# Attention, soft MoE and SoLU on one core: second weights of four late experts summed in one PSUM tile per column block

## The chip, the cores and the metric

The kernel runs on one NeuronCore of one Trainium2 chip. The metric is the device time of one execution in microseconds (us). Five engines work side by side, each through its own list of instructions in order: TensorE (PE in the profile, with its weight loads apart as PEld), VectorE (DVE), ScalarE (ACT), GpSimd (POOL) and SyncE (SP), which issues nearly all the DMAs. They wait for each other through semaphores.

## The reference

Three stages on 8 x 576 = 4608 tokens of width 512 (8 heads of 64).

```python
def sm_attn(qq, kk, vv):                       # softmax attention
    ...
p_packed = sm_attn(p, k, v)                    # 32 packed rows per head
out = sm_attn(q, p_packed, p_packed)           # x: 4608 x 512

logits = x @ phi                               # 4608 x 32, 8 experts x 4 slots
d = softmax(logits, axis=0)                    # dispatch, over the tokens
slot_input = d.T @ x                           # 32 x 512
for e in range(8):
    h = np.maximum(slot_input[e] @ w1[e], 0.0) # 4 x 1024
    slot_out[e] = h @ w2[e]                    # 4 x 512
x = softmax(logits, axis=1) @ slot_out         # 4608 x 512

h = x @ w_in                                   # 4608 x 1024
solu = h * softmax(h)
out = (layer_norm(solu) * g_ln) @ w_out        # 4608 x 512
```

w1 and w2 are 8 x 512 x 1024 and 8 x 1024 x 512 in fp32, 33.5 MB together. w_in and w_out come in 64-bit numbers and are unpacked on the chip.

## The kernel before

It has three stages. In the first, the two attentions run batch by batch while k, v, q and the first weights stream in; it ends with `SIT`, the dispatched slot inputs (line 923), which needs the maximum and the sum over all tokens and so the last batch. The second stage computes the experts. In the third, 36 tiles of 128 tokens go through w_in, the SoLU, the layer norm and w_out.

**Loads.** All bulk loads go through SP's one queue in a fixed order: k, v, q and w_in by batch, then expert weights with w_out among them. Expert weights come as 29 tiles of 128 x 2304 fp32 (1152 KB), each of nine "granules" of 128 x 256 (128 KB); 256 granules hold w1 and w2 of the eight experts. Tile 27 is loaded in three pieces (`CUTS`, line 222) and the last, tile 28, has four granules. Tiles sit in a ring of 14 buffers and a second ring of 3. A load is issued when PE has read the tile that was in its buffer. The order of the granules is set in `_layout` (lines 1649 to 1654): w1 of expert 0, then w1 of e+1 and w2 of e for e = 0 to 4, w1 of 6 and 7, and last w2 of experts 5, 6 and 7 in another arrangement: four column blocks k of 128 columns, in each block the four granules of each of the three experts.

**Experts.** `mk_w1` (line 1000) multiplies `SIT` by the 16 granules of w1 of an expert (L1008), ACT applies the relu (L1019, `hs`), PE transposes it (L1024) and ACT copies it out (L1028, `hT`, 128 x 2 x 4 x 32: all 32 slots are carried through each expert, and only the expert's own four are used in the end). `mk_w2` (line 1044) does the second product for experts 0 to 4 (L1055), copies the PSUM tile to `so` (L1066), transposes it (L1070) and copies the four slot columns into `SO` (L1039). The last NL = 3 experts go through `mk_block` (line 1084) for each block k and expert e: eight matmuls into a PSUM tile of its own (L1097), a copy to `so` on ACT (L1108), a small matmul that transposes, sums four partition groups and picks the expert's four slots (L1114, 128 x 4 columns), and after the third expert a copy of the 12 columns into `SO` (L1039). An fp32 matmul of the program shows as two instructions in the trace.

**SO times w_in.** `sw = SO @ w_in` is summed over four 128-row chunks c into two PSUM tiles n (L1317); chunk c waits for block k = c of the late experts. Then ACT and DVE write `swr` (L1325, L1329), and stage three begins with L1381. In stage three a tile costs PE 16 matmuls on L1520 and 8 on L1526.

**What sets the order.** The instructions of stages one and two are put in order by `Plan`, a list scheduler: every step has an estimated length, dependencies and buffers that it takes and gives back (`caps`, line 256: `w` are four PSUM banks, `h` the `hT` buffers). It tries 250 random variations of the priorities and keeps the best by a weighted sum of three planned times (lines 1342 to 1344). Any change of a step or a latency so gives another order in the whole of stages one and two. Matmuls of zeros (L374) fill PE where the plan sees it idle before `sw` begins.

Of the kernel before, what the change touches and what calls it, by code (L numbers as in the profile page):

```python
# [9 lines left out]
FP32 = mybir.dt.float32  # L10
# [11 lines left out]
class Plan:  # L22
# [10 lines left out]
        "PE": {"PE": 30, "DVE": 200, "ACT": 200},  # L33
# [146 lines left out]
def pack_attention__soft_moe__solu_kernel(  # L180
# [39 lines left out]
    NL = 3  # L220
# [20 lines left out]
    with ExitStack() as p12, tc.manual_schedule():  # L241
# [15 lines left out]
                     "h": 4, "u": 2, "x": 3, "c3": 1}, LOOK1, CALM1, REST1)  # L257
# [691 lines left out]
        def phase2():  # L949
# [6 lines left out]
            W["sw"] = [wp.tile([96, 512], FP32R, name=f"swr{n}") for n in range(2)]  # L956
# [3 lines left out]
            W["SO"] = wp.tile([128, 4, 3, 32], FP32, name="SO")  # L960

        def phase3():
# [3 lines left out]
            W["lo"] = wp.tile([128, 8, 512], FP16, name="wlo")  # L966

# [9 lines left out]
        def first(e):  # L977
            return max(0, 32 * e - 16) if e < NE - 1 else LATE - 16
# [7 lines left out]
        def stream(g0, g1, pe, ns, deps, acq, rel):  # L986
# [11 lines left out]
            return deps[0]  # L998

        def mk_w1(e):  # L1000
# [25 lines left out]
            def act2():  # L1026
                hT = hT_t[e] = W["k"].tile([128, 2, 4, 32], FP32, tag="hT", name="hT", bufs=4)
                nc.scalar.copy(  # L1028
                    hT, ps_t.pop(("ht", e))[:, 0:256].rearrange("p (j g s) -> p j g s", j=2, g=4)
                )  # L1030

            x = stream(first(e), first(e) + 16, pe, NS1, [o_2, o_w1.get(e - 1)], ["w", "h"], [])
            o_w1[e] = x
            x = op("ACT", 264, act, [x], rel=["w"])
            x = op("PE", 214, tr, [x], acq=["w"])
            o_hT[e] = op("ACT", 330, act2, [x], rel=["w"], urgent=10 ** 5)
# [7 lines left out]
        def mk_w2(e):  # L1044
# [19 lines left out]
            def act():  # L1064
                so_t[e] = W["k"].tile([128, 128], FP32, tag="so", name="so", bufs=3)
                nc.scalar.copy(so_t[e], ps_t["s", e][:, 0:128])  # L1066
# [11 lines left out]
            x = op("ACT", 200, act, [x], rel=["w"])  # L1078
            x = op("PE", 107, tr, [x], acq=["w"])
# [4 lines left out]
        def mk_block(k, e, dep):  # L1084
            s0 = LATE + 4 * (NL * k + e - NE + NL)

            def pe(g0, g1):
                def go():
                    if g0 == s0:
                        ps_t["b", k, e] = bank()  # L1090
                    for i in range(g0, g1):
                        for c in range(2):
# [5 lines left out]
                                out=ps_t["b", k, e][32 * a:32 * a + 32, 0:128],  # L1098
                                lhsT=hT_t[e][:, j, g, :],
                                rhs=gran(i)[:, 128 * c:128 * c + 128],  # L1100
                                start=(q == 0),
                                stop=(q == 1),
# [3 lines left out]
            def act():  # L1106
                so_t["b", k, e] = W["k"].tile([128, 128], FP32, tag="so", name="so", bufs=3)
                nc.scalar.copy(so_t["b", k, e], ps_t.pop(("b", k, e))[:, 0:128])  # L1108

            def tr():  # L1110
                if e == NE - NL:
# [575 lines left out]
```

## Time and profile before

| | us |
|---|---|
| time, median of 3 runs | 403.19 (402.27 to 403.28) |
| span of the profiled execution | 400.4 |
| PE busy in it | 379.8 (95%) |
| DVE, ACT, POOL busy | 272.8, 234.5, 209.5 |

The profile shows one more execution, of which only the span is given, from its first to its last instruction; the median of the runs is 2.8 us longer. Times in the trace count from the span's start. By them stage two begins at about 128 us and stage three at about 185 us. The DMA engines are busy throughout until about 175 us of the span, at about 410 GB/s.

### The profile page before, as it was taken

Reading aid. Unit: us, or ns where it says so; the run is one execution under the profiler, and the core shown is the slowest. Engines: PE = TensorE matmul, PEld = TensorE weight load, DVE = VectorE, ACT = ScalarE, POOL = GpSimd, SP = SyncE. Lnnn points to the kernel's source line nnn. Section 1 sums busy time; section 2 is a strip of 40 time slices with the busy share of each in tenths; the row PEclk is TensorE's granted clock in tenths of the full one; section 3 lists DMA queues with packets and bytes.
Section 4 is the critical chain, followed back from the end, with each engine's and each line's share of the span. In section 5 each row is a group of like instructions: output and inputs, shape, how many; then the busy total and the mean of one; then the engine's idle time right before and its main releaser. Section 6 shows DMA issues by size and latency. Waiting matters only on the chain.

```text
span 400.4 us, 9700 instructions
## 1 busy us (share of the span) xinstructions
PE 379.8 (95%) x3788; PEld 200.1 (50%) x3788; DVE 272.8 (68%) x562; ACT 234.5 (59%) x444; POOL 209.5 (52%) x310
## 2 busy tenths in 40 slices
PE   8889899989989999799999999999999999999996
PEld 3456455565545675453444444444444444444445
DVE  1267889689976826945987766767767676676631
ACT  1457777868645743324986656665566566655620
POOL 1024536055331583693778665566665765667540
DMA  8999999999999999950167855776556665767572
GB/s 300 410 419 406 418 410 415 411 418 414 407 419 410 407 420 419 418 199 1 33 145 160 164 133 129 140 152 153 133 118 150 138 139 121 156 148 127 121 157 80
DMA packets 91438, 99.28 MB, mean 248 GB/s; under 512 B 76160, under 2 KB 76800, under 8 KB 85888
## 3 DMA queue, kind: packets, MB, share of 16 engines
q1 hardware_dynamic: 91104, 98.58, 75.8%
q8 instruction: 30, 0.49, 0.5%
q14 instruction: 16, 0.13, 0.1%
q10 hardware_dynamic: 288, 0.07, 0.1%
HBM read 70.85 MB, written 9.44 MB: 201 GB/s over the span
## 4 chain that ended last, share of the span: by engine, by line
PE 71%; DMA 12%; DVE 10%; ACT 3%; issue 2%; SPq 1%; POOL 1%; DVEq 0%; ACTq 0%; POOLq 0%
PE o L1520 29%; PE o L1526 14%; DMA r<-w 5%; PE h L1381 4%; DMA r<-kT 3%; DMA r<-qT 3%; PE sc L390 3%; PE w L1008 3%; PE sw L1317 2%; PE w L374 2%; PE w L473 2%; PE w L1097 2%; DVE bsum L582 2%; DVE bmx L562 2%; PE w L1055 1%
## 5 line engine op out<-in xcount | busy, mean ns | idle before, releaser
L1520 PE MATMUL o<-whi,th 128*128 128x512 f16 x280 | 106.1, 379 | 0.4 <-DMA th<-hi 0.3
L1520 PE MATMUL o<-wlo,th 128*128 128x512 f16 x280 | 106.1, 379 | 0.0
L1490 POOL TENSOR_TENSOR lo<-x,hi 128x1024 f16<-128x1024 f32 (+1 forms) x37 | 77.3, 2092 | 29.8 <-ACT hi L1468 28.1
L1520 PEld LDWEIGHTS <-th 128*128 128x128 f16 x560 | 54.6, 98 | 66.4 <-DMA th<-hi 0.8
L1526 PE MATMUL o<-whi,tl 128*128 128x512 f16 x280 | 66.5, 380 | 0.0
L1430 ACT ACTIVATE e<-s3t,nv 128x1024 f32<-128x1024 f32 x36 | 41.3, 1148 | 40.1 <-DVE nmean L1424 40.0
L1468 ACT ACTIVATE hi<-s3t,nr,rs 128x1024 f16<-128x1024 f32 x35 | 43.4, 1240 | 24.2 <-POOL nr L1451 24.0
L1411 DVE SCALAR_TENSOR_TENSOR s3t<-h,e 128x1024 f32<-128x1024 f32 (+1 forms) x37 | 43.9, 1190 | 17.4 <-ACT e L1402 17.3
L1389 DVE TENSOR_REDUCE nm<-h 128x1 f32<-128x1024 f32 (+1 forms) x37 | 43.9, 1190 | 11.5 <-PE h L1381 11.4
L1460 DVE TENSOR_SCALAR x<-s3t,nmean,rs 128x1024 f32<-128x1024 f32 x35 | 28.8, 824 | 25.4 <-POOL rs L1447 25.3
L1402 ACT ACTIVATE e<-h,nm 128x1024 f32<-128x1024 f32 (+1 forms) x37 | 39.9, 1079 | 5.7 <-DVE nm L1389 3.3
L1526 PEld LDWEIGHTS <-tl 128*128 128x128 f16 x280 | 24.9, 98 | 34.3 <-issue 8.3
L1381 PE MATMUL h<-swr,cT 96*128 96x512 f32 x72 | 28.9, 483 | 1.2 <-DVE swr L1329 0.9
L374 PE MATMUL w<-wz 128*128 128x512 f16 x91 | 26.3, 379 | 3.9 <-ACT A2T L638 1.2
L1548 DVE TENSOR_TENSOR ob<-o,winv 128x512 f32<-128x512 f32 x35 | 23.9, 684 | 6.8 <-PE o L1526 6.8
L1008 PE MATMUL w<-r,SIT 128*32 128x256 f32 x256 | 21.8, 384 | 2.0 <-DMA r<-w 2.0
L594 POOL TENSOR_TENSOR A<-A,bsum 128x512 f32<-128x512 f32 (+1 forms) x18 | 18.0, 1012 | 10.7 <-DVE bsum L586 5.7
L448 POOL TENSOR_SCALAR r<-s 128x1 f32<-128x1 f32 x16 | 3.8, 237 | 34.3 <-ACT a L415 34.0
L1447 POOL TENSOR_TENSOR rs<-rs,half 128x1 f32<-128x1 f32 x36 | 20.2, 560 | 2.8
L410 DVE TENSOR_REDUCE nb<-sc 128x1 f32<-128x576 f32 x16 | 11.6, 750 | 14.5 <-PE sc L390 14.5
L1446 POOL TENSOR_TENSOR rs<-V,w 128x1 f32<-128x1 f32 x36 | 7.5, 209 | 25.7 <-ACT e L1430 25.6
L415 ACT ACTIVATE a<-sc,nb 128x576 f32<-128x576 f32 x16 | 11.8, 741 | 14.2 <-DVE nb L410 14.1
(201 smaller groups left out, 644.7 us busy)
## 6 DMA issues: line engine op xcount, KB each, us to landing
r<-w SPq DMA_DIRECT2D x27, 1152.0 KB, 15.1
r<-kT SPq DMA_DIRECT2D x16, 576.0 KB, 13.1
r<-v SPq DMA_DIRECT2D x8, 1152.0 KB, 13.9
r<-qT SPq DMA_DIRECT2D x16, 576.0 KB, 14.7
out<-ob SPq DMA_DIRECT2D x31, 256.0 KB, 2.3
r<-w_in SPq DMA_DIRECT2D x4, 1024.0 KB, 13.9
r<-w_out SPq DMA_DIRECT2D x4, 1024.0 KB, 20.8
r<-w SPq DMA_DIRECT2D x3, 512.0 KB, 17.1
```

The costliest lines, as they stand in the source:

```text
L374: nc.tensor.matmul(out=t[:, 0:FN], lhsT=wz[:, 0:128], rhs=wz[:, 0:FN], start=True, stop=True)
L1008: nc.tensor.matmul(out=hp[32 * g:32 * g + 32, 0:256], lhsT=SIT[:, k, :], rhs=gran(i), start=(k == 0), stop=(k == 3),)
L1381: nc.tensor.matmul(out=w, lhsT=cT[:, t, :], rhs=swr[n], start=True, stop=True)
L1389: nc.vector.tensor_reduce(out=z["nm"][:, h:h + 1], in_=hcols(h), axis=AX.X, op=ALU.max, negate=True)
L1402: nc.scalar.activation(out=z["e"][:, cols(h)], in_=hcols(h), func=ACTF.Exp, bias=z["nm"][:, 0:1], accum_out=z["S"][:, h:h + 1],)
L1411: nc.vector.scalar_tensor_tensor(out=z["s"][:, cols(h)], in0=hcols(h), scalar=1.0, in1=z["e"][:, cols(h)], op0=ALU.mult, op1=ALU.mult, acc ...
L1430: nc.scalar.activation(out=z["e"], in_=z["s"], func=ACTF.Square, bias=z["nv"], scale=2.0 ** -15, accum_out=z["V"])
L1460: nc.vector.tensor_scalar(out=z["x"][:, cols(h)], in0=z["s"][:, cols(h)], scalar1=z["n"], scalar2=z["r"], op0=ALU.add, op1=ALU.mult,)
L1468: nc.scalar.activation(out=z["hi"][:, cols(h)], in_=z["s"][:, cols(h)], func=ACTF.Identity, scale=z["r"], bias=z["nr"])
L1490: nc.gpsimd.tensor_tensor(out=z["lo"][:, cols(h)], in0=z["x"][:, cols(h)], in1=z["hi"][:, cols(h)], op=ALU.subtract)
L1520: nc.tensor.matmul(out=z["o"], lhsT=z["th"][:, c, :], rhs=w[:, c, :], start=(c == 0 and w is whi), stop=False)
L1526: nc.tensor.matmul(out=z["o"], lhsT=z["tl"][:, c, :], rhs=whi[:, c, :], start=False, stop=(c == 7))
```

## The change

NL goes from 3 to 4, so w2 of expert 4 also comes in the late arrangement: its granules move from before w1 of expert 6 to the end of the stream, and w1 of experts 5, 6 and 7 comes 16 granules earlier. The late experts get `hz`, a buffer of zeros that POOL fills once at the start of stage two, and only the expert's own four slot columns are copied into it. With zeros elsewhere, the products of the four experts add up in one PSUM tile per block k. So the copy to `so` and the small matmul, now of 16 columns, run once per block and no longer once per block and expert. The buffers `hT`, `hs` and `so` become two each and are counted in the plan; the `swr` buffers move to memory that is opened later in the stage. The planned latency between two PE steps goes from 30 to 0 ns.

```diff
@@ -30,7 +30,7 @@
 
 
     LAT = {
-        "PE": {"PE": 30, "DVE": 200, "ACT": 200},
+        "PE": {"PE": 0, "DVE": 200, "ACT": 200},
         "DVE": {"DVE": 127, "ACT": 130, "PE": 210, "Pool": 155},
         "ACT": {"ACT": 200, "PE": 220, "DVE": 140, "Pool": 65},
         "Pool": {"Pool": 100, "DVE": 70, "ACT": 75, "PE": 150},
@@ -217,7 +217,7 @@
     NOWN = 2
     WO_AT = 4
     NS1, NS2, NS3 = 122, 125, 142
-    NL = 3
+    NL = 4
     LATE = 32 * NE - 16 * NL
     CUTS = {27: (0, 1, 5, 9)}
     RING2 = (("w", 5), ("w", 6), ("w", 7))
@@ -254,7 +254,7 @@
 
         phi_sb = at.tile([128, 4, 32], FP32, name="phi_sb", bufs=1)
         plan = Plan({"ring": RING, "ring2": 0, "sc": 2, "w": 4, "v": 0, "a": 4, "aT": 2, "grp": 5, "ST": 1, "A2": 2, "A2T": 1, "d": 1, "T": 1,
-                     "h": 4, "u": 2, "x": 3, "c3": 1}, LOOK1, CALM1, REST1)
+                     "h": 2, "hs": 2, "so": 2, "u": 2, "x": 3, "c3": 1}, LOOK1, CALM1, REST1)
         now = [0]
 
         def op(*args, urgent=0, **kw):
@@ -953,17 +953,18 @@
             wp = ctx.enter_context(tc.tile_pool(name="wp", bufs=1, reuse_waits="tile"))
             W["k"] = ctx.enter_context(tc.tile_pool(name="hk", bufs=2, reuse_waits="tile"))
             W["inv"] = wp.tile([128, 512], FP32, name="winv")
-            W["sw"] = [wp.tile([96, 512], FP32R, name=f"swr{n}") for n in range(2)]
             W["ga"] = wp.tile([128, 8, 128], BF16, name="ga")
             W["chi"] = wp.tile([128, 9, 128], FP32R, name="chi")
             W["cT"] = wp.tile([96, NT, 128], FP32R, name="cT")
             W["SO"] = wp.tile([128, 4, 3, 32], FP32, name="SO")
+            W["hz"] = wp.tile([128, NL, 2, 4, 32], FP32, name="hz")
 
         def phase3():
             p02.close()
             wp = ctx.enter_context(tc.tile_pool(name="wp2", bufs=1, reuse_waits="tile"))
             W["hi"] = wp.tile([128, 8, 512], FP16, name="whi")
             W["lo"] = wp.tile([128, 8, 512], FP16, name="wlo")
+            W["sw"] = [wp.tile([96, 512], FP32R, name=f"swr{n}") for n in range(2)]
 
         o_2 = op("none", 1, phase2, [o_cT[u] for u in range(NU)] + [o_SIT], lat=0, rel=["v", "v"])
 
@@ -975,7 +976,7 @@
 
 
         def first(e):
-            return max(0, 32 * e - 16) if e < NE - 1 else LATE - 16
+            return max(0, 32 * e - 16) if e <= NE - NL else LATE - 16 * (NE - e)
 
         def second(e):
             return 32 * e + 32
@@ -996,6 +997,11 @@
                     o_r2.extend(deps)
                 i = j
             return deps[0]
+
+        def hz_zero():
+            nc.gpsimd.memset(W["hz"], 0.0)
+
+        o_hz = op("Pool", 700, hz_zero, [o_2])
 
         def mk_w1(e):
             def pe(g0, g1):
@@ -1024,16 +1030,20 @@
                     nc.tensor.transpose(t[:, 128 * j:128 * j + 128], hs_t[e][:, 128 * j:128 * j + 128], ident)
 
             def act2():
-                hT = hT_t[e] = W["k"].tile([128, 2, 4, 32], FP32, tag="hT", name="hT", bufs=4)
-                nc.scalar.copy(
-                    hT, ps_t.pop(("ht", e))[:, 0:256].rearrange("p (j g s) -> p j g s", j=2, g=4)
-                )
-
-            x = stream(first(e), first(e) + 16, pe, NS1, [o_2, o_w1.get(e - 1)], ["w", "h"], [])
+                t = ps_t.pop(("ht", e))[:, 0:256].rearrange("p (j g s) -> p j g s", j=2, g=4)
+                if late:
+                    hT_t[e] = W["hz"][:, e - NE + NL]
+                    nc.scalar.copy(hT_t[e][:, :, :, 4 * e:4 * e + 4], t[:, :, :, 4 * e:4 * e + 4])
+                else:
+                    hT_t[e] = W["k"].tile([128, 2, 4, 32], FP32, tag="hT", name="hT")
+                    nc.scalar.copy(hT_t[e], t)
+
+            late = e >= NE - NL
+            x = stream(first(e), first(e) + 16, pe, NS1, [o_2, o_w1.get(e - 1)], ["w"] if late else ["w", "h"], [])
             o_w1[e] = x
-            x = op("ACT", 264, act, [x], rel=["w"])
-            x = op("PE", 214, tr, [x], acq=["w"])
-            o_hT[e] = op("ACT", 330, act2, [x], rel=["w"], urgent=10 ** 5)
+            x = op("ACT", 264, act, [x], acq=["hs"], rel=["w"])
+            x = op("PE", 214, tr, [x], acq=["w"], rel=["hs"])
+            o_hT[e] = op("ACT", 240 if late else 330, act2, [x, o_hz], rel=["w"], urgent=10 ** 5)
 
         def so_out(s0, s1, k0, k1, src):
             nc.scalar.mul(
@@ -1062,7 +1072,7 @@
                 return go
 
             def act():
-                so_t[e] = W["k"].tile([128, 128], FP32, tag="so", name="so", bufs=3)
+                so_t[e] = W["k"].tile([128, 128], FP32, tag="so", name="so")
                 nc.scalar.copy(so_t[e], ps_t["s", e][:, 0:128])
 
             def tr():
@@ -1075,8 +1085,8 @@
 
             s0 = second(e)
             x = o_w2[e] = stream(s0, s0 + 16, pe, NS2, [o_hT[e], o_w2.get(e - 1)], ["w"], ["h"])
-            x = op("ACT", 200, act, [x], rel=["w"])
-            x = op("PE", 107, tr, [x], acq=["w"])
+            x = op("ACT", 200, act, [x], acq=["so"], rel=["w"])
+            x = op("PE", 107, tr, [x], acq=["w"], rel=["so"])
             o_SOT[e] = op("ACT", 280, act2, [x], rel=["w"], urgent=10 ** 5)
 
 
@@ -1086,8 +1096,8 @@
 
             def pe(g0, g1):
                 def go():
-                    if g0 == s0:
-                        ps_t["b", k, e] = bank()
+                    if g0 == s0 and start:
+                        ps_t["b", k] = bank()
                     for i in range(g0, g1):
                         for c in range(2):
                             q, r = divmod(i - s0, 2)
@@ -1095,38 +1105,35 @@
                             g, j = divmod(f, 2)
                             a = 2 * r + c
                             nc.tensor.matmul(
-                                out=ps_t["b", k, e][32 * a:32 * a + 32, 0:128],
+                                out=ps_t["b", k][32 * a:32 * a + 32, 0:128],
                                 lhsT=hT_t[e][:, j, g, :],
                                 rhs=gran(i)[:, 128 * c:128 * c + 128],
-                                start=(q == 0),
-                                stop=(q == 1),
+                                start=(start and q == 0),
+                                stop=(end and q == 1),
                             )
                 return go
 
             def act():
-                so_t["b", k, e] = W["k"].tile([128, 128], FP32, tag="so", name="so", bufs=3)
-                nc.scalar.copy(so_t["b", k, e], ps_t.pop(("b", k, e))[:, 0:128])
+                so_t["b", k] = W["k"].tile([128, 128], FP32, tag="so", name="so")
+                nc.scalar.copy(so_t["b", k], ps_t.pop(("b", k))[:, 0:128])
 
             def tr():
-                if e == NE - NL:
-                    ps_t["bt", k] = bank()
-                c0 = 4 * (e - NE + NL)
+                ps_t["bt", k] = bank()
                 nc.tensor.matmul(
-                    out=ps_t["bt", k][:, c0:c0 + 4], lhsT=so_t["b", k, e], rhs=e4[:, 4 * e:4 * e + 4], start=True, stop=True
+                    out=ps_t["bt", k][:, 0:4 * NL], lhsT=so_t["b", k], rhs=e4[:, 4 * (NE - NL):4 * NE], start=True, stop=True
                 )
 
             def act2():
                 so_out(4 * (NE - NL), 4 * NE, k, k + 1, ps_t.pop(("bt", k))[:, None, 0:4 * NL])
 
-            end = e == NE - 1
-            y = stream(s0, s0 + 4, pe, NS3, [dep, o_hT[e], o_w2[NE - NL - 1]], ["w"], ["h"] if k == 3 else [])
-            x = op("ACT", 200, act, [y], rel=["w"])
-            x = o_bt[k, e] = op("PE", 165, tr, [x, o_bt.get((k, e - 1))], acq=["w"] if e == NE - NL else [])
+            start, end = e == NE - NL, e == NE - 1
+            y = stream(s0, s0 + 4, pe, NS3, [dep, o_hT[e], o_w2[NE - NL - 1]], ["w"] if start else [], [])
             if end:
+                x = op("ACT", 200, act, [y], acq=["so"], rel=["w"])
+                x = op("PE", 165, tr, [x], acq=["w"], rel=["so"])
                 o_SOT["k", k] = op("ACT", 230, act2, [x], rel=["w"], urgent=10 ** 5)
             return y
 
-        o_bt = {}
         for e in range(NE):
             mk_w1(e)
             if e < NE - NL:
@@ -1648,8 +1655,8 @@
     q = q.reshape(8, 8, 576, 64)
     w1 = x["moe_w1"].reshape(8, 4, 128, 4, 256).transpose(0, 1, 3, 2, 4).reshape(8, 16, 128, 256)
     w2 = x["moe_w2"].reshape(8, 8, 128, 2, 256).transpose(0, 1, 3, 2, 4).reshape(8, 16, 128, 256)
-    late = x["moe_w2"][5:].reshape(3, 4, 2, 128, 4, 128).transpose(4, 0, 1, 3, 2, 5).reshape(48, 128, 256)
-    w12 = [w1[0]] + [a for e in range(5) for a in (w1[e + 1], w2[e])] + [w1[6], w1[7], late]
+    late = x["moe_w2"][4:].reshape(4, 4, 2, 128, 4, 128).transpose(4, 0, 1, 3, 2, 5).reshape(64, 128, 256)
+    w12 = [w1[0]] + [a for e in range(4) for a in (w1[e + 1], w2[e])] + [w1[5], w1[6], w1[7], late]
     w12 = np.concatenate(w12 + [np.zeros((5, 128, 256), w1.dtype)]).reshape(29, 9, 128, 256)
     w12 = w12.transpose(0, 2, 1, 3).reshape(29, 128, 2304)
     r = {
```

Line numbers of the changed kernel are 6 to 10 higher from w1 on (L1008 becomes L1014, L1097 becomes L1107, L1114 becomes L1122, L1317 becomes L1324). The scheduler's new order, at three places:

PE, end of stage two, before: the last two experts' blocks of k = 3 and the rest of `sw`.

```order
L1097 MATMUL w<-r,hT 32x128 x8
L1114 MATMUL w<-e_61,so 128x4
L1097 MATMUL w<-r,hT 32x128 x8
L1114 MATMUL w<-e_61,so 128x4
L1317 MATMUL sw<-wif,SO 96x512
L1114 MATMUL w<-e_61,so 128x4
L1317 MATMUL sw<-wif,SO 96x512 x4
```

The same place now, from the small matmul of k = 1 on.

```order
L1122 MATMUL w<-e_61,so 128x16
L1107 MATMUL w<-r,hz 32x128 x18
L1324 MATMUL sw<-wif,SO 96x512 x2
L1107 MATMUL w<-r,hz 32x128 x28
L1122 MATMUL w<-e_61,so 128x16
L1107 MATMUL w<-r,hz 32x128 x8
L1324 MATMUL sw<-wif,SO 96x512
L1107 MATMUL w<-r,hz 32x128 x8
L1324 MATMUL sw<-wif,SO 96x512
L1122 MATMUL w<-e_61,so 128x16
L1324 MATMUL sw<-wif,SO 96x512 x2
```

There are four small matmuls in all where twelve stood; one follows each block, and three of the four chunks of `sw` stand between the blocks.

DVE, end of the first stage, before: the last normalised probabilities (A), and the row maximum `mu` of the last logits.

```order
L569 TENSOR_TENSOR A_1926<-w,bmx 128x256
L594 TENSOR_TENSOR A_1926<-A_1926,bsum 128x512
L582 TENSOR_REDUCE bsum<-A_1926 128x8
L586 TENSOR_SCALAR bsum<-bsum 128x8
L590 RECIPROCAL bsum<-bsum 128x8
L594 TENSOR_TENSOR A_1926<-A_1926,bsum 128x256
L679 TENSOR_REDUCE mu<-w 128x1
L680 TENSOR_TENSOR M<-mu,M 128x1
```

The same place now.

```order
L590 RECIPROCAL bsum<-bsum 128x16 x2
L594 TENSOR_TENSOR A_1880<-A_1880,bsum 128x512
L590 RECIPROCAL bsum<-bsum 128x8
L594 TENSOR_TENSOR A_1880<-A_1880,bsum 128x256
L1201 SCALAR_TENSOR_TENSOR wif<-wif,r 128x512 x2
L1208 SCALAR_TENSOR_TENSOR wif<-r,wif 128x512 x2
L679 TENSOR_REDUCE mu<-w 128x1
L680 TENSOR_TENSOR M<-mu,M 128x1
```

Four unpacking steps of w_in (`wif`) now stand between the last A and `mu`; before, the last such steps (L1194, L1201) stood ahead of `mu` of the third of the four batch pairs. Of the fourth pair's five groups, all had their maximum (L562) and subtraction (L569) behind the third pair's `mu`; now the first group has them ahead of it.

DVE, the last steps before `SIT`, before: the global maximum (L877, L880), then the combine weights (`lt` to `ct`), then the correction `df`.

```order
L877 TENSOR_REDUCE A2T<-w 1x32
L880 COPY A2T<-A2T 1x128
L717 STREAM_TRANSPOSE lt<-ls 128x32
L719 TENSOR_REDUCE cm<-w 128x8
L720 TENSOR_REDUCE cm<-lt 128x1
L721 TENSOR_TENSOR ct<-w,cm 128x256
L724 TENSOR_SCALAR ct<-lt,cm 128x32
L891 TENSOR_TENSOR df<-M,w 128x1
```

The same place now.

```order
L717 STREAM_TRANSPOSE lt<-ls 128x32
L719 TENSOR_REDUCE cm<-w 128x8
L720 TENSOR_REDUCE cm<-lt 128x1
L721 TENSOR_TENSOR ct<-w,cm 128x256
L724 TENSOR_SCALAR ct<-lt,cm 128x32
L877 TENSOR_REDUCE A2T<-w 1x32
L880 COPY A2T<-A2T 1x128
L731 TENSOR_REDUCE cs<-ct 128x9
```

The two steps of the global maximum have moved behind the five of the combine weights, and the three `cs` steps ahead of `df`.

Stage three stands in the same order as before on DVE, ACT, POOL and SP; on PE there are three more fill matmuls.

## Rows read from the trace of the kernel before

**Rows 1.** The page: its first line.

```profile
span 400.4 us, 9700 instructions
```

**Rows 2.** Stretches: busy us (instructions) of PE, PEld, DVE, ACT, POOL; clock, DMA share, GB/s.

```profile
128.00:150.00 22.00, 22.00 (x435) 14.81 (x433) 13.96 (x18) 12.34 (x23) 14.73 (x12) 1.00 1.00 409
158.00:168.00 10.00, 6.92 (x97) 3.99 (x100) 9.64 (x14) 3.15 (x8) 4.62 (x5) 1.00 1.01 418
168.00:177.40 9.40, 9.40 (x134) 5.30 (x130) 6.50 (x6) 2.27 (x9) 9.40 (x10) 1.00 0.77 307
177.40:185.00 7.60, 6.97 (x63) 3.42 (x55) 0.69 (x1) 2.33 (x7) 5.94 (x6) 1.00 0.01 2
```

**Rows 3.** Chain that ended last, 147 to 186 us: start, length, what.

```profile
148.04 19.40 DMA r<-w
...
167.57 1.08 PE w L1097 x32
...
178.91 0.57 PE w L1097 x16
179.48 0.32 PE w L1114 x2
179.80 0.94 PE sw L1317 x2
...
180.85 3.53 PE sw L1317 x8
```

**Rows 4.** PE's groups from 166 to 185 us: count, busy us, mean ns.

```profile
L1097 PE MATMUL w<-r,hT 128*32 128x128 f32 x162 | 7.4, 278 | 0.6 <-DMA r<-w 0.6
L1114 PE MATMUL w<-e,so 128*128 128x4 f32 x24 | 4.3, 254 | 0.0
```

**Rows 5.** Issue on SP (start, us) and us to landing: tile 26, then tile 28.

```profile
150.73 0.33 SPq L307 DMA_DIRECT2D r<-w  x1
...
r<-w SPq DMA_DIRECT2D x1, 1152.0 KB, 22.7
...
161.91 0.33 SPq L307 DMA_DIRECT2D r<-w  x1
...
r<-w SPq DMA_DIRECT2D x1, 512.0 KB, 15.5
```

**Rows 6.** ACT in order of time, the end of stage two.

```profile
179.60 0.27 ACT L1108 COPY so<-w 128x128 f32<-128x128 f32 x1 [0.62 <-PE w L1097]
180.89 0.20 ACT L1039 ACTIVATE SO<-w 128x36 f32<-128x36 f32 x1 [1.02 <-PE w L1114]
```

**Rows 7.** SP's long wait before tile 13, its landing; landing of the first 128 KB.

```profile
SPq L307 <- PE w L1008: 16.3, 1, 16.3
...
129.37 0.33 SPq L307 DMA_DIRECT2D r<-w  x1
...
r<-w SPq DMA_DIRECT2D x1, 1152.0 KB, 6.0
...
p_sb<-pT SPq DMA_DIRECT2D x1, 128.0 KB, 2.5
```

**Rows 8.** DVE in order of time, the last batch pair of stage one.

```profile
100.78 0.68 DVE L1201 SCALAR_TENSOR_TENSOR wif<-r,wif 128x512 uint32<-128x512 uint32 x1
...
104.02 1.28 DVE L569 TENSOR_TENSOR A<-w,bmx 128x512 f32<-128x512 f32 x2
...
118.98 0.46 DVE L679 TENSOR_REDUCE mu<-w 128x1 f32<-128x288 f32 x1 [2.26 <-PE w L664]
...
122.13 0.42 DVE L721 TENSOR_TENSOR ct<-w,cm 128x256 f32<-128x256 f32 x1
...
127.51 0.29 DVE L923 COPY SIT<-w 128x128 f32<-128x128 f32 x1 [0.84 <-PE w L917]
```

**Rows 9.** POOL in order of time, around the start of stage three.

```profile
177.72 5.62 POOL L1299 TENSOR_TENSOR wlo<-r,whi 128x512 f16<-128x512 f32 x5
188.78 0.19 POOL L1438 TENSOR_TENSOR S<-S 128x1 f32<-128x1 f32 x1 [5.44 <-ACT e L1402]
```

## The prediction

> **What bounds the kernel now.** I read the chain of waits first, then the stretches, then the places where the change moves work. The span is 400.4 us [rows 1]; the profiled execution's own time is not given, and the median of the runs, 403.19, is 2.8 us more. I make the sum against the span and carry the 2.8 us over unchanged.
>
> Up to 167.44 us the chain is loads: tile 24 of the expert weights lands then (148.04 + 19.40) [rows 3]. The DMA engines are full from 128 to 168 us, 409 and 418 GB/s at a share of 1.00 and 1.01 [rows 2], so nothing on an engine can bring a landing forward; a late issue can only push it back. From 158 to 168 us PE keeps up with the loads: it is busy for 6.92 of 10 us [rows 2] and waits for a tile before 167.57 [rows 4]. Then this turns round. From 168 to 177.4 us PE is busy for 9.40 of 9.40 us while the DMA share falls to 0.77 [rows 2]. Tile 26 lands at 150.73 + 22.7 = 173.4 and tile 28, the last, at 161.91 + 15.5 = 177.4 [rows 5], but PE is through with the blocks only at 179.48 and with `sw` at 180.85 + 3.53 = 184.38 [rows 3]. So the end of stage two is PE's backlog, 7.0 us behind the last load. Stage three is PE's from its pipeline's filling on, and the change leaves it alone; I let it move as a whole with the end of `sw`.
>
> **The change part by part.**
>
> *What PE had to do after 167.57.* The 16.8 us up to 184.38 are 160 of the block instructions at 0.57/16 = 0.036 us (5.7), ten pairs of the small matmul at 0.32 (3.2) and eight pairs of `sw` at 0.94 (7.5) [rows 3]; that makes 16.4, and the missing 0.4 are seams between them.
>
> *What it has to do now.* Expert 4 adds 64 block instructions (2.3 us), but the stream is as long as before, and from tile 24 on it still holds 40 granules, so 160 instructions. The added ones lie in tiles 21 to 23, where PE has time to spare. Block k = 0 now ends with granule 207, the first of tile 23, instead of granule 219 in tile 24. Its small matmul and one pair of `sw` stand in the new order ahead of the wait for tile 24, so three small pairs (1.0) and seven pairs of `sw` (6.6) are left: 5.7 + 1.0 + 6.6 = 13.3 us, and 180.9 if PE never waited.
>
> *The last loads now count.* I followed the new order against the landings of the profile. Tile 25 lands about halfway between 24 and 26, at 170.4. Its 36 instructions (1.3) and two pairs of `sw` (1.9) keep PE until 173.6, about when tile 26 lands. Tile 26 takes 1.3, to 174.9. Tile 27 comes in three pieces between 173.4 and 177.4; its last four granules, at about 176.2, take 0.6, to 176.8, with the small matmul of k = 2 done before them. One pair of `sw` follows (177.8). Then the last four granules, landed at 177.4: 0.57 (178.4). The second `sw` pair of chunk 2 (179.3) covers the last copy on ACT, 0.27 [rows 6]. Then the last small pair, 0.32 (179.6), the copy into `SO`, 0.20 [rows 6] and about 0.2 for the two hand-overs (180.0), and the two `sw` pairs of chunk 3, 1.88: 181.9 against 184.38. **That is 2.5 us less.**
>
> Bounds. A matmul with 16 columns on a 128 x 128 weight is not in the trace. The nearest row has 4 columns and costs 0.32 a pair, the next has 512 and costs 0.94 [rows 3]; only the last one is on the path, so it adds 0 to 0.6, and I take 0 since the weight load is the same. The best case is a last block that finds PE free and no second `sw` pair ahead of the small matmul: 177.4 + 0.1 + 0.57 + 0.5 + 0.32 + 0.4 + 1.88 = 181.2, a gain of 3.2. With 0.6 for the wide matmul, and 0.7 more of seams and hand-overs, the gain is 1.2.
>
> *Edits that I cost at nothing.* The eight copies to `so` that go (0.27 each) [rows 6] ran on ACT beside PE. The fill of `hz` has no row; it lies between 0 and 2.2 us (two of POOL's 128 x 512 steps at 5.62/5) [rows 9]. POOL is idle for 7.3 of the 22 us from 128 to 150 [rows 2], and the first reader is the late experts' copy some 20 us on; without that cover it would hold up w1's transposes by its length. Fewer `hT` buffers make PE do w2 of an expert before w1 of the next but one, which is the order in which the granules land. POOL's last step for w_out ends at 177.72 + 5.62 = 183.3 and its next work came at 188.78 [rows 9]; with the shift it comes at 186.3, so 3 us are left there.
>
> *The new order of stage one.* It matters through one wait. SP waited 16.3 us for PE's first w1 matmuls before it could issue tile 13, and that tile landed 6.0 us after its issue [rows 7]. Its 1180 KB take 2.9 us at 409 GB/s, and a transfer of 128 KB that waits for nothing needs 2.5, so 2.2 without its own 0.3; that leaves 0.9 us in which SP may be later before the DMA engines run dry. What the order does to `SIT` (127.51) [rows 8]: one group's maximum and subtraction go ahead of the third pair's `mu`, -1.28 on a DVE that is then the chain. Four unpacking steps of 0.6 to 0.7 fill the 2.26 us in which DVE waited for PE before the last `mu`, +0.2 to 0.4. The global maximum goes behind five steps of up to 0.42, so +1 to 2, of which I take 1.1. In sum 0, with some 1.5 us either way, of which only lateness over 0.9 us counts.
>
> So the span goes to 397.9 and the time to 403.19 - 2.5 = **400.7 us**.
>
> **The rivals.**
>
> *Loads run dry (ends slower).* The place is the issue of tile 13. If `SIT` comes d later than at 127.51, every later landing moves by d - 0.9, and the end of stage two with it. The gain is gone at d = 3.4, and the kernel is slower by over 0.3% (1.2 us, about what a measurement here can tell from no change) from d = 4.6. At d = 2.5 the time is 402.3, at d = 5.5 it is 405.3. For it speaks that the whole order of stage one is another; against it that the two shifts on DVE nearly cancel. I give 0.20 to a d between 2 and 4.6 and 0.08 to more.
>
> *The clock falls (slower).* PE will wait for loads more often up to 177 us. [...] Chance 0.03.
>
> *The gain is eaten on the way (same).* The last block's chain of copy, matmul and copy is exposed now, and so are ACT's queue and POOL's, where 3 us of slack remain. Each hand-over 0.3 us dearer than I take it, with the wide matmul at its upper bound, or the w_out steps over 3 us later on POOL, leaves 402 to 403. Chance 0.09.
>
> *More than that.* The best case above, or a stream without its small stumbles: 399 to 400. Chance 0.06.
>
> **How the numbers follow.** My forecast, 399.9 to 401.9, has 0.54; loads somewhat late 0.20, much late 0.08, the clock 0.03, eaten 0.09, more 0.06. Faster by over 0.3%, under 402.0: 0.54 + 0.06 and a fifth of the loads somewhat late, 0.64. Slower, over 404.4: 0.08 + 0.03, rounded to 0.12. Same: 0.24. The range goes from 399.6 to 403.6: it leaves out the slower cases and about 0.07 below and between.
>
> **What would show it.** In the profile of the changed kernel: the last expert tile lands within 0.5 us of 177.4, or else loads ran dry; PE waits for DMA before tiles 25 to 28, where before it had no idle time; four small matmuls (eight instructions) of some 0.32 a pair; `sw` ends at about 181.9 and the first stage-three matmul follows it as closely as before, so some 2.5 us earlier than there; the clock stays at 1.00. The forecast is wrong if the first w1 matmul starts later than about 129 us, or if stage three's start does not move with `sw`.

## The result, and the profile after

The changed kernel took 406.04 us (median of 12 runs, 403.47 to 407.37); the kernel before, beside it on the same chip, 402.42 (12 runs). The ratio is **1.0081, with a 95% interval of 1.0063 to 1.0098**: slower by 3.3 us, where I had forecast 2.5 us less. Ratios and intervals, here and below, are taken over all executions of both kernels, so they can differ by 0.001 or 0.002 from the quotient of two medians. The profiled execution is the longest (407.37, with a span of 405.6), so its times serve to find places, and the medians to weigh them.

The stretches of [rows 2] in the changed kernel (busy us and instructions of PE, PEld, DVE, ACT, POOL; granted clock, DMA share, GB/s):

```profile
128.00:150.00 22.00, 21.29 (x420) 13.82 (x417) 18.48 (x29) 13.82 (x25) 11.72 (x10) 1.00 0.90 362
158.00:168.00 10.00, 6.89 (x110) 3.82 (x100) 9.76 (x15) 3.33 (x8) 4.28 (x4) 1.00 1.01 418
168.00:177.40 9.40, 8.51 (x104) 5.46 (x108) 8.88 (x9) 0.95 (x4) 8.05 (x7) 0.64 1.02 415
```

Two things differ from before. From 128 to 150 us the DMA engines are no longer full (0.90 instead of 1.00): loads ran dry. And from 168 us PE works at a mean granted clock of 0.64, where before it was 1.00.

SP's waits from 100 to 140 us (total, times, longest), then the issue of tile 13 with its start and its time to landing, which answer to [rows 7]:

```profile
SPq L307 <- PE w L1014: 13.1, 3, 12.1
...
133.88 2.09 SPq L307 DMA_DIRECT2D r<-w  x3
...
r<-w SPq DMA_DIRECT2D x1, 1152.0 KB, 5.3
```

Tile 13 goes out at 133.88 instead of 129.37. The last expert tile lands at 180.96 instead of 177.43 (read from each tile's issue and time to landing, as in [rows 5]).

The chain that ended last, which answers to [rows 3] (start, length, what):

```profile
150.36 18.18 DMA r<-w
...
168.59 2.35 PE w L1107 x36
...
181.91 0.57 PE w L1107 x16
...
185.11 0.14 PE w L1122 x2
185.28 0.22 ACT SO L1049
...
185.54 1.97 PE sw L1324 x4
```

The 36 block instructions at 168.59 took 2.35 us, where 36 at a granted clock of 1.00 take 1.22 to 1.28. `sw` ends at 187.51, 3.1 us later than before. Stage three then takes 212.6 to 213.8 us from there to the last matmul in all twelve kernels profiled here, before included (212.9): it moves as a whole to within 1.2 us, as I had assumed.

### The profile page after: what moved, and what is told of

It reads as the page before. It is cut to its first block, busy times and chain, and to the rows that moved or that the text cites. A ratio compares the mean times of both kernels' runs of the same rounds, so it can differ in the third digit from the quotient of the medians.

```text
span 405.6 us, 9657 instructions
## 1 busy us (share of the span) xinstructions
PE 376.3 (93%) x3777; PEld 199.4 (49%) x3777; DVE 281.6 (69%) x562; ACT 231.3 (57%) x434; POOL 210.5 (52%) x311
## 4 chain that ended last, share of the span: by engine, by line
PE 65%; DMA 17%; DVE 9%; ACT 3%; issue 3%; POOL 2%; SPq 0%; ACTq 0%; DVEq 0%; POOLq 0%
PE o L1527 28%; PE o L1533 14%; DMA r<-w 7%; DMA r<-w_in 4%; DMA r<-kT 3%; PE h L1388 3%; PE sc L390 3%; PE sw L1324 2%; PE w L1107 2%; DMA p_sb<-pT 2%; PE o L1540 1%; PE w L1014 1%; DVE s3t L1418 1%; PE w L473 1%; DVE nm L1396 1%
## 5 line engine op out<-in xcount | busy, mean ns | idle before, releaser
L374 PE MATMUL w<-wz 128*128 128x512 f16 x94 | 26.3, 380 | 0.7 <-DVE A L569 0.4
L473 PE MATMUL w<-r,aT 128*32 128x64 f32 (+1 forms) x640 | 15.1, 223 | 4.4 <-issue 3.9
L1014 PE MATMUL w<-r,SIT 128*32 128x256 f32 x256 | 17.4, 381 | 1.2 <-DMA r<-w 1.2
## 6 DMA issues: line engine op xcount, KB each, us to landing
r<-w_in SPq DMA_DIRECT2D x4, 1024.0 KB, 14.5
r<-w_out SPq DMA_DIRECT2D x4, 1024.0 KB, 14.7
```

What stands on the lines that cost most here:

```text
L374: nc.tensor.matmul(out=t[:, 0:FN], lhsT=wz[:, 0:128], rhs=wz[:, 0:FN], start=True, stop=True)
```

## Experiments

To test an order apart from the planner's search, several kernels have it written out: for each engine a list of the planner's steps by number (HOLD), which the planner then follows. The lists are left out below.

**The old stage one under the new tail.** On top of the changed kernel:

```
-        plan.trials = 250
+        plan.trials = 0
+        plan.hold = HOLD
```

> The changed kernel with every engine's order up to the end of stage one written out as it was before; from there on each engine keeps the order of the changed kernel. Theory (the loss is the new stage-one order, which made tile 13 go out at 133.88 instead of 129.37 and the last expert tile land at 180.96 instead of 177.43): tile 13 goes out at 129.4, the last tile lands within 0.5 us of 177.4, sw ends at 181.9 as I had predicted, and the time is 2.5 us below that of the kernel before, so about 399.9. Rival A (the new tail itself loses, by waits and the granted clock that fell to 0.50 from 168 to 175 us): the loads are back, but the clock falls in this kernel too, sw ends at 184 or later and the time is 402 to 404. Rival B (something else in stage two makes the loads late): the last tile lands at 180 or later again, 405 to 406.

Measured: 402.37 us against 402.89, ratio 0.9975 (0.9954 to 0.9995). By the marks of the expectation this is rival A's number, 402 to 404, and not the theory's 399.9. The executions spread from 399.62 to 403.63, and the spread goes with the mean granted clock that each shows: the three at 1.000 took 399.62 to 400.26, as the theory wants; the other nine, at 0.990 to 0.999, took 401.05 to 403.63. The profiled one is not among the three: it lost the clock at 91 us, in stage one, and held it in the tail, which is not what rival A says. Tile 13 went out at 131.83 and the last tile came at 179.93, so the theory's 129.4 and 177.4 are not to be seen in it. Where the other eight lost the clock no trace tells. The chain shows what the tail does after the loads:

```profile
161.79 16.89 DMA r<-w
...
178.72 0.64 PE w L1115 x16
...
182.00 0.14 PE w L1130 x2
...
182.43 1.97 PE sw L1332 x4
```

`sw` ends 184.40 - 179.93 = 4.47 us after the last landing. My sum had 181.9 - 177.4 = 4.5. So the tail does what was forecast behind its last load, and what moves that load lies ahead of it.

**The new stage one under the old tail.** The reverse, on the kernel before.

> The kernel before (three late experts, a small matmul for each) with every engine's order up to the end of stage one written out as it is in the changed kernel; from there on its own order. Theory: tile 13 goes out at about 133.9, the last tile lands at about 181, PE's backlog of 7.0 us behind it stays, sw ends at about 187.9 and the time is 3.5 us above the kernel before, about 406; if the granted clock falls as well, up to 2 us more. Rival (the lateness comes from the change in stage two): last tile at 177.4, time 402.4.

Measured: 407.11 us, ratio 1.0103 (1.0083 to 1.0124). Tile 13 went out at 134.75, the last tile landed at 181.79 and `sw` ended at 188.97, 7.2 us behind it (7.0 before). The stage-one order alone makes the kernel slower by at least as much as the whole change does (four executions, each with some of the clock lost, 0.992 to 0.996). The rival that put the lateness down to stage two falls.

**Work for PE while it waits.** In the changed kernel, its own order written out, with 20 more warming matmuls (L374) in front of tiles 20 to 23.

> The changed kernel, its own order on every engine, with 20 more warming matmuls (128 x 512 on zeros, 0.22 us each) on PE in four groups of five, where PE waits for tiles 20 to 23 (157 to 168 us). They stand ahead of waits that last 1.2 us or more per tile, so they should delay nothing. Theory (the clock fell because PE stood idle over half of 162 to 168 us): the granted clock stays at 1.00 up to 190 us, sw ends at about 185.5 instead of 187.5, the last tile lands at 181 as before, and the time is 2 us below the changed kernel's, about 404. Rival (the clock's fall has another reason, or costs nothing since the last loads end the stage anyway): sw at 187.5 and the time of the changed kernel, 406.

Measured: 403.87 us, ratio 1.0023 (1.0007 to 1.0039), against 1.0081 without them: 2.3 us. First the kernel before in the stretches ahead of the fall of the clock, then the changed kernel there and in the fall, then the one with the fills:

```profile
162.00:164.00 2.00, 1.69 (x19) 0.62 (x17) 1.90 (x3) 0.25 (x1) 1.31 (x2) 1.00 1.03 429
164.00:166.00 2.00, 1.31 (x34) 1.14 (x34) 1.82 (x4) 0.60 (x2) 0.58 (x1) 1.00 0.98 410
166.00:168.00 2.00, 1.35 (x24) 1.18 (x26) 2.00 (x3) 0.69 (x3) 1.15 (x2) 1.00 1.00 419
```

```profile
162.00:164.00 2.00, 1.24 (x31) 1.02 (x31) 2.00 (x2) 0.94 (x2) 1.99 (x2) 1.00 1.02 424
164.00:166.00 2.00, 1.03 (x22) 0.76 (x23) 1.93 (x4) 0.73 (x3) 0.13 (x1) 1.00 1.01 424
166.00:168.00 2.00, 0.84 (x28) 0.58 (x20) 1.82 (x4) 0.00 (x0) 1.08 (x1) 1.00 1.00 405
168.00:170.00 2.00, 1.42 (x28) 1.30 (x32) 1.89 (x4) 0.27 (x1) 0.73 (x1) 0.57 1.03 429
170.00:172.00 2.00, 1.70 (x19) 1.15 (x12) 2.00 (x2) 0.21 (x1) 1.92 (x3) 0.50 1.01 419
```

```profile
158.00:168.00 10.00, 9.73 (x118) 4.92 (x110) 9.25 (x14) 3.07 (x8) 3.90 (x4) 1.00 1.01 421
168.00:176.00 8.00, 7.70 (x122) 4.75 (x121) 7.86 (x8) 0.95 (x4) 6.47 (x6) 1.00 1.00 409
```

Without fills PE was busy for about half of 162 to 168 us, and then the granted clock was 0.50 until about 175. With them PE was busy for 9.73 of 10 us and the clock stayed at 1.00; `sw` ended at 185.06, 4.6 us after a last landing at 180.50, where it had ended 6.5 us after it. The profiled execution is at 1.00 throughout; seven of the twelve still show 0.990 to 0.996, and where they lost it no trace tells.

**Another draw, from the kernel before.** `"PE": {"PE": 30` becomes `"PE": {"PE": 0`, nothing else.

> The kernel before with one number of the change alone: the planner's 30 ns between two PE steps set to 0, which makes its random search end at another order for stages one and two (neither the one of before nor that of the changed kernel). Theory (what the search draws for stage one sets the time by the issue of tile 13, by some us either way): the time differs from that of the kernel before by the shift of the last landing, which follows the issue of tile 13 as (issue - 129.4 - 0.9) where positive; I expect between 0 and +4 us, 402 to 406, as the old draw left only 0.9 us. Rival (the planner's orders are all about as good, and the loss came from the new tail): within 0.8 us of the kernel before.

Measured: 403.40 us, ratio 1.0005 (0.9988 to 1.0022). In its trace `SIT` comes at 129.59, tile 13 goes out at 131.45 and the last tile lands at 178.81; `sw` ends at 184.91, 0.5 us later than before. The landing moved by 1.4 us as theory has it (2.1 - 0.9 = 1.2), but the time hardly, since this draw's PE backlog behind it is 6.1 us instead of 7.0. By its mark the rival is met (within 0.8 us), and the theory's sentence that the time follows the landing is not; but the new tail is not in this kernel, so that the loss came from there does not follow.

**Both repairs together.** The changed kernel with the stage-one order of before and the 20 fills.

> Both repairs together: the changed kernel with the stage-one order of before and 20 warming matmuls on PE in front of tiles 20 to 23. Theory (three separate things: the new tail saves 2.5 us, the stage-one order costs 3.5 us, the fall of the granted clock in the tail costs 2 us): the clock stays at 1.00 from 150 to 190 us, sw ends 4.5 us behind the last landing, at about 182, and the median is about 400.2 us, ratio 0.994 to the kernel before; single executions may still lose the clock for some us in stage one, as some of the kernel before do. Rival (the fills delay the tail as much as the clock did, or the fall of the clock hardly counts): 402.4 us, as without the fills.

Measured: **400.37 us against 403.19, ratio 0.9935 (0.991 to 0.996)**, the best of all; below this is the repaired kernel. Six of eight executions show a clock of 1.000 and took 399.18 to 401.30. The profiled one is one of the other two: the clock fell in stage one (92 to 95 us), yet held in the tail.

**Half of the change: four late experts, no common tile.** On the repaired kernel, in `mk_block`:

```
-                        ps_t["b", k] = bank()
+                        ps_t["b", k, e] = bank()
...
-                                start=(start and q == 0),
-                                stop=(end and q == 1),
+                                start=(q == 0),
+                                stop=(q == 1),
```

and with it a copy and a small matmul for each expert.

> One half of the change alone: four late experts, w1 of 5 to 7 early, rows in hz, but for each expert and column block its own PSUM tile, copy and small matmul, as before (16 pairs instead of 4). Stage-one order of before and the same fills; the tail's order is the planner's. Theory (the end of stage two is PE's backlog from tile 24 on: 160 block instructions 5.7 us, 12 or 13 small pairs at 0.32, seven sw pairs 6.6): it ends at about 184, so 0.3 to 0.5 us below before at most, 402.4 us. Rival (what counts is that the w1 matmuls and expert 4 lie earlier, not the small matmuls): as the run with the summed tile, 400.2.

Measured: 402.12 us against 403.19, ratio 0.9983 (0.9965 to 1.0001). Its chain has no load in it at the end, though the last tile landed at 176.91:

```profile
180.06 0.57 PE w L1115 x16
180.64 0.32 PE w L1132 x2
180.95 0.94 PE sw L1335 x2
...
182.01 2.67 PE sw L1335 x6
```

That ends at 184.68 (the expectation had about 184, the kernel before has 184.38): PE's backlog again, with a small pair after every block. The theory holds: without the common tile hardly anything is gained.

**The other half: three late experts, summed.** On the repaired kernel `NL = 3` and the weight order of before.

> The other half alone: still three late experts (the weight order of before), but summed in one PSUM tile for each column block, from rows that are zero outside the expert's slots. Stage-one order of before and the same fills. Theory (backlog from tile 24 on: 160 block instructions 5.7 us, four small pairs 1.3, eight sw pairs 7.5, so 182.1 against a bound of 181.9 from the last landing): sw ends at about 182.3 and the time is at most 0.5 us above that of four summed experts, about 400.5. Rival (the fourth late expert is needed to bring the gain): 401.5 or more.

Measured: 401.80 us against 403.19, ratio 0.9968 (0.9947 to 0.9988), so about half of the gain, which is the rival's mark. `sw` ended at 183.14, not 182.3. The chain shows where the difference begins:

```profile
167.99 0.38 PE w L1038 x2
...
168.63 1.28 PE w L1115 x36
...
180.48 2.66 PE sw L1332 x6
```

The backlog begins at 168.63 instead of 167.57, behind the last expert's transposes (L1038) and its copy to `hz`. But the kernel before has these transposes too, at 166.11. What is new is ahead of them. Tile 23 landed at 164.65 before and at 164.61 here; the first matmul on it, before and then here with what PE did until then:

```profile
164.69 0.40 PE L1008 MATMUL w<-r,SIT 128*32 128x256 f32 x1 [1.00 <-DMA r<-w]
```

```profile
165.10 1.47 PE L382 MATMUL w<-wz 128*128 128x512 f16 x6
166.50 0.40 PE L1022 MATMUL w<-r,SIT 128*32 128x256 f32 x1
```

Here it is the warming matmuls, placed for four late experts, that make PE 1.8 us late. From the start of the backlog the sum held, 14.5 us against 14.7. So this run does not show that the fourth late expert is needed; no run had three summed experts without these fills.

**Another draw of the changed kernel.** The planner's 0 put back to 30.

> The changed kernel with the planner's number for two PE steps put back to 30 ns, which makes the search end at another order for stages one and two. Theory (the stage-one order is what costs the changed kernel its gain, and it is a matter of the draw): SIT is written somewhere between 127 and 133 us, and the time lies 4.5 us plus the following stage three behind the last landing, which follows SIT; between 400.5 and 407, with about 404 as the middle. Rival (the new number of 30 or 0 itself is what made stage one late, since it lets the planner think PE faster than it is): stage one is as before, SIT at 127.5, and the time is that of the run with the old stage-one order, 402.4.

Measured: 401.32 us against 403.19, ratio 0.9951 (0.993 to 0.9972), five executions, all at a clock of 0.999 or 1.000. `SIT` came at 128.48, the last tile at 178.42, and `sw` ended at 183.48, 5.1 us after it. The same change under another draw is faster by half a percent, without any repair. That lies in the theory's range, near its lower end; the order is not that of before, as the rival had it. What the two runs with another draw leave open is whether the number itself does harm: `SIT` came at 127.51 and 128.48 with 30, and at 129.59 and 132.02 with 0 (the 129.59 with a fall of the clock at 93 us). With two draws of each, that can't be told from chance.

**Which part of stage one.** The repaired kernel again, once with the early part of stage one (to the second pair's `mu`) in the old order and the rest in the new, once the other way round.

> Everything as in the repaired kernel (new tail, fills), but of stage one only the part up to the second pair's maximum mu stands in the order of before; from there to its end it is the order of the changed kernel. In the traces that mu came at 73.3 us before and 76.0 in the changed kernel, the fourth's at 119.0 and 122.0, SIT at 127.5 and 132.0. Theory (the delay is made mostly in the first 76 us, where I had not looked, and handed on): mu at about 73, SIT at about 129.3 where the granted clock holds, the loads about 1 us late, about 401.5 us. Rival (the later part makes it, as I had taken for granted when I costed only that part): SIT at 131 or later, 403 or more.

> The other way round: stage one in the changed kernel's order up to the second pair's mu, then in the order of before. Theory: mu at about 76, SIT at about 130.2 (127.5 and 2.7), loads about 1.8 us late, about 402 us. Rival (the later part makes the delay, and the early one is caught up again): SIT at 128.5 or earlier, 400.5.

Measured, against 402.33: early part old 400.91 us, ratio 0.9984 (0.9964 to 1.0005); early part new 403.24, 1.0016 (1.0001 to 1.0031). `mu` of the second and fourth pair and `SIT` on DVE, first with the early part old, then with it new:

```profile
73.17 0.46 DVE L687 TENSOR_REDUCE mu<-w 128x1 f32<-128x288 f32 x1 [0.56 <-PE w L672]
...
119.62 0.46 DVE L687 TENSOR_REDUCE mu<-w 128x1 f32<-128x288 f32 x1 [0.70 <-PE w L672]
...
129.62 0.29 DVE L931 COPY SIT<-w 128x128 f32<-128x128 f32 x1 [1.17 <-PE w L925]
```

```profile
75.38 0.46 DVE L687 TENSOR_REDUCE mu<-w 128x1 f32<-128x288 f32 x1 [0.67 <-PE w L672]
...
121.72 0.46 DVE L687 TENSOR_REDUCE mu<-w 128x1 f32<-128x288 f32 x1 [2.26 <-PE w L672]
...
130.26 0.29 DVE L931 COPY SIT<-w 128x128 f32<-128x128 f32 x1 [0.84 <-PE w L925]
```

Against 127.51 [rows 8] the early part makes 2.75 us of lateness and the later part 2.11; together 4.9, where the changed kernel has 4.51. Both rivals fall, and both parts count. Which counts for more is not shown: where the whole old order ran without a fall of the clock, `SIT` came between 127.19 and 127.98, so 0.6 us is within the spread.

## Why the prediction was wrong

**The tail: right.** The backlog did turn into a wait for the last loads, as the chain of the run with the old stage one shows. The end of `sw` 4.5 us after the last landing was measured as 4.47 and 4.6, and the repaired kernel gains 0.65% (2.6 us) against the 2.5 forecast. It has 20 warming matmuls that the change has not; without them, the three executions with the old stage one at a clock of 1.000 gain 2.6 to 3.3 us on the median of the kernel before. The matmul with 16 columns costs what I took: 0.34 a pair in the run with the early part old, against 0.32 for four columns [rows 3]. The fill of `hz` took 0.95 us on POOL, inside its bounds.

**The step that failed is the sum for `SIT`: "In sum 0, with some 1.5 us either way".** `SIT` came 4.5 us later. Here are the rows, first the second pair's `mu` in the kernel before, then the same in the changed one:

```profile
73.30 0.46 DVE L679 TENSOR_REDUCE mu<-w 128x1 f32<-128x288 f32 x1 [0.56 <-PE w L664]
```

```profile
76.01 0.46 DVE L679 TENSOR_REDUCE mu<-w 128x1 f32<-128x288 f32 x1 [0.67 <-PE w L664]
```

Then the fourth, and the end, in the changed kernel:

```profile
122.00 0.46 DVE L679 TENSOR_REDUCE mu<-w 128x1 f32<-128x288 f32 x1 [0.69 <-PE w L664]
122.49 0.97 DVE L680 TENSOR_TENSOR M<-mu,M 128x1 f32<-128x1 f32 x1
...
132.02 0.29 DVE L923 COPY SIT<-w 128x128 f32<-128x128 f32 x1 [1.17 <-PE w L917]
```

Up to the second `mu`, from there to the fourth `mu`, and from there to `SIT`, the lateness is 2.7 + 0.3 + 1.5 = 4.5 us:

*Up to the second `mu`* I had nothing. I costed only what moved on DVE in the last 30 us of stage one and left the start unmoved, so this term was missing, not mis-sized. It is not a step of DVE either. The chain that leads to this `mu` in the changed kernel holds two stops of PE for which the profile shows no wait:

```profile
63.76 1.37 issue
...
72.22 1.28 issue
...
74.77 1.18 PE w L664 x16
```

Together they are 2.65 of the 2.71 us. The other three profiles with the new early part have both (1.37 and 1.01 or 1.02); the eight with another one have no stop of PE over 0.8 us there up to 76 us. Why PE stops, the last section asks.

*From the second to the fourth `mu`* I had -1.28 and +0.2 to 0.4, so about 1 us less. It took 45.99 us instead of 45.68. The group that goes ahead of the third `mu` saved nothing.

*From the fourth `mu` to `SIT`* I had taken 1.1 of "+1 to 2": 8.53 us before, 10.0 now, so 1.5. That this comes near is luck, for 0.81 of it is the step `M` above, 0.97 us instead of 0.16, which I had not in the sum.

The planner itself saw none of it: by its numbers `SIT` moved by 0.6 us and the second pair's `mu` not at all. Counting places in an order, as I did, is as blind to such stops as that.

**Loads run dry: the rival that came.** Its formula held for this kernel: 4.5 - 0.9 = 3.6 us, and the last tile came 3.53 later, which gives 404.3. A d of 4.5 lies at the upper end of the stretch to which I gave 0.20, and its time above my range. The formula is not general: with the old stage one and in the other draw of the changed kernel the last tile came 2.50 and 0.99 us late at a d of 2.46 and 0.97 by tile 13, so by all of d. Nor does stage one matter "through one wait". In the changed kernel the loads had already run dry at 110 to 112 us (DMA share 0.33, before 0.98): the load that went out at 108.39 before went out at 111.16, and tile 12 landed 1.65 us later. Tile 13 was later still, so its wait is the one that counted here.

**The clock falls: it came as well.** I gave it 0.03 because PE at 69% of 158 to 168 us had kept 1.00 [rows 2]; a fall, and what it costs, no row of before shows. Over the same ten microseconds the changed kernel is at 69% too, but at 0.84 to 1.24 of each 2 us from 162 on, where before it was at 1.31 to 1.69; the mean over ten hid it. PE waited 0.82, 0.97 and 1.74 us for tiles, and in the last of these waits the granted clock fell to 0.50, from 168.3 to 175.1 us. What exactly makes it fall is not shown: with the old stage one PE was at 1.65, 1.29 and 0.59 us in the same three stretches, and the clock held. The price by the run with fills is 2.3 us.

The sum is -2.5 + 3.6 + 2.3 = 3.4 us; measured, 0.0081 x 402.42 = 3.3. I had treated the two rivals as apart, but the late landings and the idle PE came together here. That the second always follows from the first isn't shown: with the new stage one under the old tail the loads were late as well, and the profiled execution lost the clock only in stage one (80 to 84 us).

## What to carry to other kernels

Where a search sets the order, an edit to one stage redraws the others: hold the old order for what is not meant to change, or take the time of several draws, before judging the edit. The change itself, and a constant of the search that is changed with it, are two edits. A feed of loads with under 1 us of margin belongs at the head of the sum, and every engine's order is to be followed from its first difference. What an order does not tell, an engine's stops and steps that take six times as long, is read off the chain in the trace. When an edit turns a backlog into a wait, look for stretches of a few microseconds where the engine will stand idle, not at a mean over ten.

## What I had not expected of the hardware

**A one-column step on DVE that takes six times as long.** The `M` step at 122.49 above took 0.97 us; the other two of this kernel, at 76.50 and 105.40 with POOL idle, take 0.16. At 122.49 POOL was multiplying two tiles:

```profile
120.79 2.65 POOL L1225 TENSOR_TENSOR wif<-wif,ux 128x512 f32<-128x512 f32 x2 [2.19 <-DVE wif L1208]
```

These two steps end at 123.44 us, and `M` at 123.46. It is no chance: seven other profiles have an `M` of 0.92 to 0.95 us, and each ends within 0.02 us of the end of such a step on POOL; with the old stage one `M` ends at 103.40 + 0.93 = 104.33 and the step at 103.14 + 1.17 = 104.31. In the changed kernel it is 0.8 us on the chain to `SIT`. Why `M` ends with the step is not shown.

**PE stands still where the profile shows no wait, and the clock may follow.** In the kernel before, in the run with the old stage one, and in the repaired one, before the same matmul:

```profile
90.54 0.71 PE L390 MATMUL sc<-r,p_sb 64*32 64x288 f32 x13 [1.67 <-issue]
```

```profile
90.27 0.71 PE L398 MATMUL sc<-r,p_sb 64*32 64x288 f32 x13 [1.95 <-issue]
...
91.46 1.91 PE L382 MATMUL w<-wz 128*128 128x512 f16 x4
```

```profile
91.12 0.71 PE L398 MATMUL sc<-r,p_sb 64*32 64x288 f32 x13 [1.95 <-issue]
...
92.46 1.91 PE L382 MATMUL w<-wz 128*128 128x512 f16 x4
```

After 1.67 us the clock stayed; after 1.95 us, twice, it fell 0.8 and 0.6 us later (four warming matmuls in 1.91 us), and `SIT` came 1.8 and 2.7 us late with nothing changed in the order (0.5 of the 2.7 was there at the second `mu`, and 0.6 of each is a long `M`). That the stop brings the fall is not shown. A stop of 1.74 us before 79.4 to 79.7 us stands in three profiles with the new stage one: the clock fell 1 us later in the one with the old tail (80.6 us), and stayed in the changed kernel and in the one with fills; in the kernel before with the planner's 0 it fell at 92.5 us after a stop of 0.95. Counted over the records, such stops of 1 to 2 us stand before PE instructions of about 2,498 and 3,010 in the kernel before, and 1,986, 2,242, 2,498 and 3,266 in the changed one (the count can be off by one or two where records start together): all apart by multiples of 256, in both orders, and with the DMA engines full (a share of 0.99 to 1.04 in these six). The first two of the changed kernel are the two on the chain to the second `mu`. The page of either kernel shows a DMA queue of the kind "instruction" (packets, MB, share of 16 engines):

```profile
q8 instruction: 30, 0.49, 0.5%
```

That is 16 KB a packet; the profiles of the two kernels hold 7,655 and 7,623 records of PE and PEld, about 255 to a packet if all of them are PE's. In the changed kernel one of these packets starts at 62.8, 71.0, 77.2 and 98.6 us, in the kernel before at 75.6 and 88.1: each stop ends 2.3 to 2.6 us after such a start. Most of the 30 packets have no such stop behind them. That PE waits for its instructions there is my estimate from these numbers, and not shown: no run moved a packet alone.
